# Expert tails in pairs of neighbouring tiles, five PSUM banks in turn, GpSimd's low parts behind VectorE's

## The chip, the cores and the metric

One core of one Trainium2 chip. The metric is the time of one execution on the device, in microseconds; the time of a kernel is the median of its runs.

## What is computed

The kernel chains three layers over 3072 tokens (4 batches of 768) of 320 features: a recurrent attention, a mixture of eight experts that gives each token to one expert, and a gated layer. The change lies in the second.

```python
x = attention output, reshaped to (3072, 320)
for e in range(8):                      # _moe_ref
    mask = expert_idx == e
    h = np.maximum(x[mask] @ w1[e], 0.0)            # 320 -> 1024
    out[mask] = gate_w[mask, None] * (h @ w2[e])    # 1024 -> 320
gate = 1.0 / (1.0 + np.exp(-(x @ w_gate)))          # _moe2_ref
return gate * (x @ w_val) @ w_out
```

## The kernel before, in words

TensorE multiplies in f16, so each f32 operand is split into a high part and a low part (the rest after the high one), and a product takes three matmuls: high by high, high by low, low by high. The program is written in one order by hand; each engine works its own queue in that order, and waits only on semaphores.

**Runs.** The experts are sorted by the number of their tokens. The list `runs` has nine entries: runs 0 and 1 are two halves of the first expert (256 tokens each), runs 2 to 8 one expert each, with windows of 512, 480, 448, 416, 384, 352 and 336 tokens. A run computes with its tokens as the moving columns. The hidden layer of 1024 is eight tiles of 128 units, f = 0 to 7. `expert_run` holds the arithmetic, `expert_steps` puts the work of the other engines between the tiles.

**Layer 1 of a tile** (`l1_tile`): 320 features are two whole blocks of 128 and a tail of 64. A whole block takes three matmuls (L1041, L1042, L1043). For the tail, `w1s` holds the 64 high rows above the 64 low rows, and `x` holds its tail twice, so that two matmuls (L1044, L1045) give all four partial products: 8 matmuls a tile. The results lie in one of PSUM banks 0, 1, 2 in turn. `hidden` then reads the bank twice: ScalarE writes `hh` (L1138), VectorE `hl` (L1139).

**Layer 2** (`expert_l2`) runs two tiles behind: 320 output features are two blocks of 128, three matmuls each (L1054 to L1056), and a tail of 64, whose high and low columns lie side by side in `w2h`, so two matmuls (L1058, L1059) with 128 output rows. `expert_out` adds the two halves of `ys[2]` and stores.

**Between the tiles.** `prepare(f)` refills weights just used with those of the next expert: `split_w1` and `split_w2` are ScalarE copies of the high parts (L221, L244, L258), a VectorE subtraction for the tail's low part (L216) and a GpSimd subtraction for the low part of the whole blocks (L247, L261). The gated layer's f64 weights are split in pieces at the same time (VectorE L1202 to L1219, GpSimd L1223). `load_x` (L767) lets GpSimd gather the token rows of the next run, one block of 128 for each of f = 0 to 3; ScalarE scales a block three tiles later (L1001). At a run's end `transpose_part` turns these rows on TensorE (L1028) into banks 6 and 7 and one of 0 to 2; only as many rows of the last block as the window has. The layer after the experts starts at L1803 with matmuls on half the array's rows (64x128), two at a time.

Of the kernel before, what the change touches and what calls it, by code (L numbers as in the profile page):

```python
# [22 lines left out]
def kernel(  # L23
# [40 lines left out]
    KS, KT, KU = 15, 4, 8  # L64
    SLO, SHI = 2.0 ** -14, 3.99
# [20 lines left out]

    def tp_ps(name):
        return next_bank((6, 7), name)
# [110 lines left out]
    def load_w1(k, p):  # L199

        t = w1r[:, p % 2]
        m, r = t[:, 0:4 * P].rearrange("p (k f) -> p k f", k=2), t[:, 4 * P:6 * P]
        w = w1[expert(k)][0][:, p * 2 * P:(p + 1) * 2 * P]
        nc.sync.dma_start(out=m, in_=w[0:2 * P].rearrange("(k p) f -> p k f", p=P))
        for u in range(2):
            nc.sync.dma_start(out=r[u * RM:(u + 1) * RM], in_=w[2 * P:DM])
        wraw[1, k, p] = (m, r)
# [19 lines left out]
    def tail_sub(dst, x, k, y, early):  # L227
        if early:
            return lambda: scaled_copy(x, x, k), lambda: nc.gpsimd.tensor_tensor(
                out=dst, in0=x, in1=y, op=ALU.subtract  # L230
            )
        return lambda: None, lambda: scaled_sub(dst, x, k, y)

    def split_w1(k, p, lo=None):
        m, r = wraw.pop((1, k, p))
        fs = slice(p * 2 * P, (p + 1) * 2 * P)
        e = lo or nc.gpsimd

        lower = slice(RM, P)
        pre, sub = tail_sub(w1s[lower, fs], r[lower], KT, w1s[lower, fs], k == 0 and lo is None)  # L240

        return [
            lambda: (scaled_copy(w1s[:, fs], r, KT), pre()),
            lambda: nc.scalar.copy(w1h[:, :, fs], m),  # L244
        ], [
            sub,
            lambda: e.tensor_tensor(out=w1l[:, :, fs], in0=m, in1=w1h[:, :, fs], op=ALU.subtract),  # L247
        ]

    def split_w2(k, p, lo=None):  # L250
# [784 lines left out]
    def l1_tile(ps, ws, xt, f):  # L1035

        hi, lo, st = ws
        h, l = xt
        fs = slice(f * P, (f + 1) * P)
        for kk in range(2):  # L1040
            nc.tensor.matmul(ps, hi[:, kk, fs], h[:, kk], start=(kk == 0), stop=False)  # L1041
            nc.tensor.matmul(ps, hi[:, kk, fs], l[:, kk], start=False, stop=False)  # L1042
            nc.tensor.matmul(ps, lo[:, kk, fs], h[:, kk], start=False, stop=False)  # L1043
        nc.tensor.matmul(ps, st[:, fs], h[:, 2], start=False, stop=False)  # L1044
        nc.tensor.matmul(ps, st[:, fs], l[:, 2], start=False, stop=True)  # L1045

    def ring(tag):
        return mw.tile([P, NM], F16, tag=tag, name=tag, bufs=3)

    def expert_l2(ys, hh, hl, f):  # L1050
        first, last = f == 0, f == NF1 - 1
        for d in range(2):
# [3 lines left out]
            nc.tensor.matmul(ys[d], wl, hh, start=False, stop=last)  # L1056
        wr = w2h[:, f, 2 * P:]
# [65 lines left out]
    def expert_run(n):  # L1123
# [326 lines left out]
    last_part, last_low = [], []  # L1450
    PIECES = ((), (), (4,), (2, 4, 6), (2, 4, 6), (2, 4), (2, 4), (4,), (4,))

    def expert_steps(n):
# [7 lines left out]
        def refill(f, u, e, p, lo=None):  # L1461

            if e < NE:
                copies, lows = (split_w1, split_w2)[u](e, p, lo)
                acts[f] += copies
                rest[f].append(lows)
                e, p = (e, p + 2) if p < 2 else (e + 1, p - 2)
                if e < NE:
                    loads[f].append(lambda: (load_w1, load_w2)[u](e, p))

        def prepare(f):
            if n == 1:
# [31 lines left out]
        for f in range(NF1):  # L1504
# [3 lines left out]
            if more and f < len(blocks(n + 1)):  # L1508
                load_x(n + 1, (f,))
# [6 lines left out]
            weave(*rest[f])  # L1516
            weave(ends[f])
# [246 lines left out]

    for n in range(2, len(runs)):
# [43 lines left out]
    sync = mybir.DependencyInfo(mybir.DependencyClass.Sync, mybir.DependencyReason.DATA)  # L1809
# [46 lines left out]
    def gated_h(t, s):  # L1856
        gh, gl = (mw.tile([P, NM], F16, tag=z, name=z, bufs=3) for z in ("hh", "hl"))
# [540 lines left out]
```

## Time and profile before

| what | us |
|---|---|
| median of 3 runs | 706.83 (705.7 to 707.31) |
| the profiled execution | 709.01 |
| its span, first to last instruction | 707.0 |
| runs 2 to 8 in that span | 166.24 to 336.17 |
| the gated layer | 336.17 to 707.0 |

The span is what the trace shows; 2.0 us of the profiled execution lie around it. TensorE is busy in 96% of the span, VectorE in 60%, ScalarE in 59% and GpSimd in 46%. A TensorE row of the trace lasts longer than the step to the next one, since matmuls are pipelined: what a matmul costs is read from start to start.

### The profile page before, as it was taken

Reading aid. Unit: us, or ns where it says so; the run is one execution under the profiler, and the core shown is the slowest. Engines: PE = TensorE matmul, PEld = TensorE weight load, DVE = VectorE, ACT = ScalarE, POOL = GpSimd, SP = SyncE. Lnnn points to the kernel's source line nnn. Section 1 sums busy time; section 2 is a strip of 40 time slices with the busy share of each in tenths; the row PEclk is TensorE's granted clock in tenths of the full one; section 3 lists DMA queues with packets and bytes.
Section 4 is the critical chain, followed back from the end, with each engine's and each line's share of the span. In section 5 each row is a group of like instructions: output and inputs, shape, how many; then the busy total and the mean of one; then the engine's idle time right before and its main releaser. Section 6 shows DMA issues by size and latency. Waiting matters only on the chain. (4 is left out here: it accounts for less than half of the span.)

```text
span 707.0 us, 17947 instructions
## 1 busy us (share of the span) xinstructions
PE 681.2 (96%) x6955; PEld 428.1 (61%) x6955; DVE 424.8 (60%) x928; ACT 419.7 (59%) x1063; POOL 328.1 (46%) x392
## 2 busy tenths in 40 slices
PE   6999999999999999999999999999999999999994
PEld 6899998885445556666555555545544555555552
DVE  7978888797789999887898873343211122211111
ACT  5887886866966677778665554455455453333332
POOL 8968888543754766674010005343243324324222
PEclk9999999999999999999999999999999999999998
DMA  7655875555445566651223211010010001001001
GB/s 231 212 190 180 276 223 160 150 170 162 138 149 177 162 197 191 197 163 57 57 84 88 63 57 40 1 39 1 2 38 2 1 2 38 2 2 39 1 2 41
DMA packets 39865, 70.47 MB, mean 100 GB/s; under 512 B 4818, under 2 KB 28460, under 8 KB 39772
## 3 DMA queue, kind: packets, MB, share of 16 engines
q1 hardware_dynamic: 36764, 59.61, 28.2%
q0 software_dynamic: 3008, 9.64, 4.2%
q8 instruction: 56, 0.92, 0.6%
q14 instruction: 37, 0.30, 0.2%
HBM read 60.55 MB, written 8.68 MB: 98 GB/s over the span
## 5 line engine op out<-in xcount | busy, mean ns | idle before, releaser
L1848 DVE SCALAR_TENSOR_TENSOR sgm<-v_ps,sgm 128x512 f32<-128x512 f32 (+1 forms) x74 | 49.9, 676 | 201.8 <-ACT sgm L1847 201.8
L1861 POOL TENSOR_TENSOR hl<-sgm,hh 128x512 f16<-128x512 f32 x54 | 62.4, 1159 | 214.2 <-ACT hh L1860 214.1
L1803 PE MATMUL v_ps<-xg,wvh 64*128 64x512 f16 x290 | 108.8, 375 | 3.9 <-ACT seen L1817 3.8
L1803 PE MATMUL g_ps<-xg,wgh 64*128 64x512 f16 x290 | 108.8, 375 | 0.0
L1804 PE MATMUL g_ps<-xg,wgh 64*128 64x512 f16 x290 | 108.6, 375 | 0.0
L1804 PE MATMUL v_ps<-xg,wvh 64*128 64x512 f16 x290 | 108.6, 375 | 0.0
L1805 PE MATMUL g_ps<-xg,wgl 64*128 64x512 f16 x290 | 108.6, 375 | 0.0
L1805 PE MATMUL v_ps<-xg,wvl 64*128 64x512 f16 x290 | 108.6, 375 | 0.0
L1847 ACT ACTIVATE sgm<-g_ps 128x512 f32<-128x512 f32 (+1 forms) x74 | 43.1, 585 | 73.1 <-PE g_ps L1805 70.4
L1884 PE MATMUL o_ps<-wo,hh 64*128 64x320 f16 x560 | 84.9, 296 | 1.4 <-ACT seen L1817 1.4
L1886 PE MATMUL o_ps<-wo,hl 64*128 64x320 f16 x560 | 84.8, 296 | 0.5 <-POOL hl L1861 0.5
L1885 PE MATMUL o_ps<-wo,hh 64*128 64x320 f16 x560 | 84.9, 296 | 0.0
L1860 ACT CAST hh<-sgm 128x512 f16<-128x512 f32 (+1 forms) x74 | 44.8, 606 | 43.2 <-DVE sgm L1848 42.2
L1817 ACT COPY seen<-zeros 1x1 f32<-1x1 f32 x142 | 26.8, 188 | 67.6 <-PE o_ps L1886 37.2
L1055 PE MATMUL y_ps<-hl,w2h 128*128 128x256 f16 (+7 forms) x144 | 46.8, 325 | 1.7 <-DVE hl L1139 1.7
L1043 PE MATMUL h_ps<-xh,w1l 128*128 128x256 f16 (+7 forms) x144 | 47.4, 329 | 0.0
L1042 PE MATMUL h_ps<-xl,w1h 128*128 128x256 f16 (+7 forms) x144 | 47.3, 329 | 0.0
L1041 PE MATMUL h_ps<-xh,w1h 128*128 128x256 f16 (+7 forms) x144 | 47.3, 328 | 0.0
L247 POOL TENSOR_TENSOR w1l<-w1raw,w1h 128x512 bf16<-128x512 f32 x31 | 37.6, 1211 | 20.8 <-ACT w1h L244 19.7
L1054 PE MATMUL y_ps<-hh,w2h 128*128 128x256 f16 (+7 forms) x144 | 46.8, 325 | 0.0
L1056 PE MATMUL y_ps<-hh,w2l 128*128 128x256 f16 (+7 forms) x144 | 46.8, 325 | 0.0
L479 PE MATMUL s_ps<-qk 40*128 40x128 f32 (+1 forms) x384 | 42.1, 300 | 4.5 <-DMA qk<-in_qkt_dram 4.3
(383 smaller groups left out, 1963.1 us busy)
## 6 DMA issues: line engine op xcount, KB each, us to landing
kv<-in_kvo_dram SPq DMA_DIRECT2D x24, 484.0 KB
w2raw<-in_moe_w_dram SPq DMA_DIRECT2D x32, 320.0 KB
w1raw<-in_moe_w_dram SPq DMA_DIRECT2D x32, 256.0 KB
qk<-in_qkt_dram SPq DMA_DIRECT2D x48, 160.0 KB
xs<-x SPq DMA_DIRECT2D x24, 192.0 KB
w1raw<-in_moe_w_dram SPq DMA_DIRECT2D x64, 64.0 KB
raw<-in_moe_w_out_dram SPq DMA_DIRECT2D x12, 320.0 KB
raw<-in_moe_w_gate_dram SPq DMA_DIRECT2D x8, 384.0 KB
```

The source lines that it names most:

```text
L1041: nc.tensor.matmul(ps, hi[:, kk, fs], h[:, kk], start=(kk == 0), stop=False)
L1042: nc.tensor.matmul(ps, hi[:, kk, fs], l[:, kk], start=False, stop=False)
L1043: nc.tensor.matmul(ps, lo[:, kk, fs], h[:, kk], start=False, stop=False)
L1054: nc.tensor.matmul(ys[d], wh, hh, start=first, stop=False)
L1803: lambda: nc.tensor.matmul(ps, at(wh), h[rows, kk], start=start, stop=False),
L1804: lambda: nc.tensor.matmul(ps, at(wh), l[rows, kk], start=False, stop=False),
L1805: lambda: nc.tensor.matmul(ps, at(wl), h[rows, kk], start=False, stop=stop),
L1848: nc.vector.scalar_tensor_tensor(out=s[:, cs], in0=pv[:, cs], scalar=2.0 ** -KH, in1=s[:, cs], op0=ALU.mult, op1=ALU.mult)
L1861: e.tensor_tensor(out=gl[:, cs], in0=s[:, cs], in1=gh[:, cs], op=ALU.subtract)
L1884: lambda: nc.tensor.matmul(o, gh[rows, ts_], wh[rows], start=begin, stop=False),
L1885: lambda: nc.tensor.matmul(o, gh[rows, ts_], wl[rows], start=False, stop=False),
L1886: lambda: nc.tensor.matmul(o, gl[rows, ts_], wh[rows], start=False, stop=end),
```

## The change

For runs 2 to 8 it multiplies the tails of two neighbouring tiles together. In `w1s` the 64 high rows of an even tile now lie above those of the odd tile, the low rows likewise in the next 128 columns, and each tile's three tail products use one half of the array's rows, the two tiles alternating (`l1_tails`). They come ahead of the tile's other products, for four tiles at once, at f = 0 and f = 4. In layer 2 the tails of two tiles use one half of the array's columns each (`l2_tails`), at f = 4 for tiles 0 and 1 and after the last tile for the rest, so `hh` and `hl` get six buffers (three before, also in the gated layer). Tiles, transposes and the small products of runs 2 to 8 take banks 0, 1, 2, 6, 7 in turn. From the third expert on each GpSimd low part waits for the VectorE subtraction recorded last. The tail's f32 rows are loaded without doubling, so its ScalarE copy handles 128x128 elements (before 128x256) and its VectorE subtraction 128x128 (before 64x256). `load_x` stands behind the tile's splits instead of ahead of them, row blocks are turned whole, and the tail of the last layer-2 refill moves into the next run (`kept`).

```diff
     def load_w1(k, p):
...
+            if k:
+                nc.sync.dma_start(out=r[rows, 0:P], in_=w[2 * P:DM, u * P:(u + 1) * P])
...
+    def holds(op):
+        port[:] = [op()]
+    def yields(ins):
+        if port:
+            tc.add_manual_dep(ins.ins, port[0].ins.name, sync, reason="VectorE goes first")
+        return ins
...
-        return lambda: None, lambda: scaled_sub(dst, x, k, y)
+        return lambda: None, lambda: holds(lambda: scaled_sub(dst, x, k, y))
+    def low_op(k, ins, e):
+        if k > 1 and e is nc.gpsimd:
+            yields(ins)
...
+        if k:
+            hi, lw = (w1s[:, (2 * p + v) * P:(2 * p + v + 1) * P] for v in range(2))
+            r = r[:, 0:P]
+            pre, sub = tail_sub(lw, r, KT, hi, False)
...
-            m = min(P, s0 + w - j * P)
-            o, xr = tp[:, u * P:u * P + m], xrow[n][0:m, u, kk * P:(kk + 1) * P]
-            nc.tensor.transpose(o, xr, ident[0:m, 0:m])
+            nc.tensor.transpose(tp[:, u * P:(u + 1) * P], xrow[n][:, u, kk * P:(kk + 1) * P], ident)
...
+    def l1_tails(pss, ws, xt, f):
+        h, l = (z[:, 2] for z in xt)
+        def three(ps, rows):
+            hi, lo = (ws[2][rows, (f + v) * P:(f + v + 1) * P] for v in range(2))
+            return [
+                lambda: nc.tensor.matmul(ps, hi, h[rows], start=True, stop=False),
+                lambda: nc.tensor.matmul(ps, hi, l[rows], start=False, stop=False),
+                lambda: nc.tensor.matmul(ps, lo, h[rows], start=False, stop=False),
+            ]
+        alternate(*(three(ps, rows) for ps, rows in zip(pss, half_rows)))
...
+    def l2_tails(ys, hs, f):
+        def three(u):
+            rows, (hh, hl) = half_rows[u], hs[u]
+            hi, lo = (w2h[:, f + u, 2 * P + v * RM:2 * P + (v + 1) * RM] for v in range(2))
+            o = ys[2][rows]
+            return [
+                lambda: nc.tensor.matmul(o, hi, hh, start=(f == 0), stop=False),
+                lambda: nc.tensor.matmul(o, hi, hl, start=False, stop=False),
+                lambda: nc.tensor.matmul(o, lo, hh, start=False, stop=(f == NF1 - 2)),
+            ]
+        alternate(three(0), three(1))
...
+                if f == 4:
+                    l2_tails(ys, [h.pop(u) for u in range(2)], 0)
+                if f % 4 == 0:
+                    for u in range(0, 4, 2):
+                        for v in range(2):
+                            pss[f + u + v] = tp_ps("h_ps")[:, 0:w]
+                        l1_tails([pss[f + u + v] for v in range(2)], ws, x, f + u)
+                l1_main(pss[f], ws, x, f, False, True)
...
+        if n > 1:
+            for f in range(2, NF1, 2):
+                l2_tails(ys, [h.pop(f + u) for u in range(2)], f)
...
-            if more and f < len(blocks(n + 1)):
-                load_x(n + 1, (f,))
             prepare(f)
...
             weave(*rest[f])
+            if more and f < len(blocks(n + 1)):
+                load_x(n + 1, (f,))
...
+    tp_banks[0] = (0, 1, 2, 6, 7)
     for n in range(2, len(runs)):
```

On TensorE, where run 2 begins, the first tile before had its tail behind the whole blocks (`w1s` is the tail's weights, `w1h` and `w1l` those of the whole blocks):

```order
L1041 LDWEIGHTS w1h
L1041 MATMUL h_ps<-xh,w1h 128x512
L1042 LDWEIGHTS w1h
L1042 MATMUL h_ps<-xl,w1h 128x512
L1043 LDWEIGHTS w1l
L1043 MATMUL h_ps<-xh,w1l 128x512
L1044 LDWEIGHTS w1s
L1044 MATMUL h_ps<-xh,w1s 128x512
L1045 LDWEIGHTS w1s
L1045 MATMUL h_ps<-xl,w1s 128x512
```

Now run 2 begins with the tails of tiles 0 and 1, of which this is the first pair:

```order
L1099 LDWEIGHTS w1s
L1099 MATMUL h_ps<-xh,w1s 128x512
L1099 LDWEIGHTS w1s
L1099 MATMUL h_ps<-xh,w1s 128x512
L1100 LDWEIGHTS w1s
L1100 MATMUL h_ps<-xl,w1s 128x512
L1100 LDWEIGHTS w1s
L1100 MATMUL h_ps<-xl,w1s 128x512
L1101 LDWEIGHTS w1s
L1101 MATMUL h_ps<-xh,w1s 128x512
L1101 LDWEIGHTS w1s
L1101 MATMUL h_ps<-xh,w1s 128x512
```

Each line stands twice, once for each tile; the third token block `xh`, `xl`, which was needed last, is needed first.

On TensorE at f = 4 of run 2, what is now between the last whole-block product of layer 2 (L1129) and the tails of tiles 4 and 5 (L1099):

```order
L1129 MATMUL y_ps<-hh,w2l 128x512
L1116 LDWEIGHTS w2h
L1116 MATMUL y_ps<-hh,w2h 64x512
L1116 LDWEIGHTS w2h
L1116 MATMUL y_ps<-hh,w2h 64x512
L1117 LDWEIGHTS w2h
L1117 MATMUL y_ps<-hl,w2h 64x512
L1117 LDWEIGHTS w2h
L1117 MATMUL y_ps<-hl,w2h 64x512
L1118 LDWEIGHTS w2h
L1118 MATMUL y_ps<-hh,w2h 64x512
L1118 LDWEIGHTS w2h
```

Six matmuls with 64 output rows each stand in a row; whole array, column halves, row halves and whole array follow one another.

On GpSimd in run 3 before, each gather of token rows (L767) stood ahead of its tile's low part (L247, L261):

```order
L767 DMA xrow<-xs,idx 128x384
L247 TENSOR_TENSOR w1l<-w1raw,w1h 128x2x256
L767 DMA xrow<-xs,idx 128x384
L261 TENSOR_TENSOR w2l<-w2raw,w2h 128x512
L767 DMA xrow<-xs,idx 128x384
L247 TENSOR_TENSOR w1l<-w1raw,w1h 128x2x256
L767 DMA xrow<-xs,idx 128x384
L261 TENSOR_TENSOR w2l<-w2raw,w2h 128x512
```

Now each stands behind it (L798 is the gather, L278 and L292 the low parts):

```order
L278 TENSOR_TENSOR w1l<-w1raw,w1h 128x2x256
L798 DMA xrow<-xs,idx 128x384
L292 TENSOR_TENSOR w2l<-w2raw,w2h 128x512
L798 DMA xrow<-xs,idx 128x384
L278 TENSOR_TENSOR w1l<-w1raw,w1h 128x2x256
L798 DMA xrow<-xs,idx 128x384
L292 TENSOR_TENSOR w2l<-w2raw,w2h 128x512
L798 DMA xrow<-xs,idx 128x384
```

So a gather waits for whatever its tile's low part waits for.

## Rows read from the trace of the kernel before

**Rows 1.** Windows, runs 5, 8: length; PE, PEld, DVE, ACT, POOL busy; clock; DMA
```profile
251.92:275.45 23.53, 23.53 (x138) 13.53 (x137) 22.94 (x36) 16.82 (x45) 15.30 (x15) 1.00 0.61 179
...
317.83:336.17 18.34, 18.34 (x130) 12.43 (x128) 12.93 (x26) 14.31 (x37) 8.45 (x8) 1.00 0.18 55
```
**Rows 2.** Timeline of TensorE, run 2, one layer-2 tile of eight matmuls: start, duration
```profile
171.52 0.38 PE L1054 MATMUL y_ps<-hh,w2h 128*128 128x512 f16 x1
...
173.24 0.38 PE L1041 MATMUL h_ps<-xh,w1h 128*128 128x512 f16 x1
```
**Rows 3.** Timeline of TensorE, end of run 8 and start of the gated layer
```profile
333.65 0.31 PE L1059 MATMUL y_ps<-hl,w2h 128*128 128x336 f16 x1
...
335.93 0.31 PE L1059 MATMUL y_ps<-hl,w2h 128*128 128x336 f16 x1
336.17 0.39 PE L1803 MATMUL g_ps<-xg,wth 64*128 64x512 f16 x1
336.18 0.39 PE L1803 MATMUL v_ps<-xg,wth 64*128 64x512 f16 x1
336.40 0.38 PE L1804 MATMUL g_ps<-xg,wth 64*128 64x512 f16 x1
```
**Rows 4.** Timeline of TensorE, attention: column halves (128x64); the x2 row: last two alone
```profile
42.49 0.27 PE L598 MATMUL tp_x<-ident,x 128*128 128x128 f32 x1
42.70 0.66 PE L529 MATMUL u_ps<-vw,kv 128*64 128x41 f32 x16
43.29 0.38 PE L479 MATMUL s_ps<-qk 128*128 128x128 f32 x1
...
43.07 0.29 PE L529 MATMUL u_ps<-vw,kv 128*64 128x41 f32 x2
```
**Rows 5.** Timeline of TensorE near the end: row halves, then the whole array
```profile
693.78 0.30 PE L1886 MATMUL o_ps<-wo,hl 64*128 64x320 f16 x2
694.01 0.31 PE L1905 MATMUL o_ps<-wo,hh 128*128 128x320 f16 x1
```
**Rows 6.** Timeline of TensorE: turning rows for run 2 (512) and run 4 (448)
```profile
160.86 1.47 PE L1028 MATMUL tp_m<-ident,xrow 128*128 128x128 f32 x12
162.17 0.27 PE L1054 MATMUL y_ps<-hh,w2h 128*128 128x256 f16 x1
...
220.56 2.05 PE L1028 MATMUL tp_m<-ident,xrow 128*128 128x128 f32 x12
222.55 0.38 PE L1054 MATMUL y_ps<-hh,w2h 128*128 128x480 f16 x1
```
**Rows 7.** Lines of VectorE, 166 to 336 us: busy us, mean ns, idle before
```profile
L216 DVE SCALAR_TENSOR_TENSOR w1s<-w1raw,w1s 64x256 f16<-64x256 f32 x25 | 18.7, 747 | 2.2 <-ACT w1s L221 1.5
```
**Rows 8.** Timeline of run 5, TensorE, VectorE and GpSimd: tile 3 from matmul to use
```profile
258.78 0.34 PE L1045 MATMUL h_ps<-xl,w1s 128*128 128x416 f16 x1
...
264.81 0.34 PE L1055 MATMUL y_ps<-hl,w2h 128*128 128x416 f16 x1
...
258.39 1.91 DVE L216 SCALAR_TENSOR_TENSOR w1s<-w1raw,w1s 64x256 f16<-64x256 f32 x1
...
264.17 0.58 DVE L1139 SCALAR_TENSOR_TENSOR hl<-h_ps,hh 128x416 f16<-128x416 f32 x1
...
266.54 0.42 DVE L216 SCALAR_TENSOR_TENSOR w1s<-w1raw,w1s 64x256 f16<-64x256 f32 x1
...
258.84 1.16 POOL L261 TENSOR_TENSOR w2l<-w2raw,w2h 128x512 bf16<-128x512 f32 x1
```
**Rows 9.** Timeline of run 5, GpSimd and ScalarE: first gather, first low part, first scaling
```profile
252.15 1.30 POOL L767 DMA_INDIRECT xrow<-xs,idx  x1
...
256.37 1.34 POOL L247 TENSOR_TENSOR w1l<-w1raw,w1h 128x512 bf16<-128x512 f32 x1
...
259.66 0.60 ACT L1001 ACTIVATE xrow<-xrow,gsl 128x384 f32<-128x384 f32 x1
```
**Rows 10.** Timeline of TensorE, end of run 2: the product that spreads the gate weights
```profile
193.36 1.12 PE L1010 MATMUL sp_ps<-dg,ones_f 128*128 128x512 f32 x2 [0.58 <-DVE xl L216]
```

More of the change, by code (lines that the diff above doesn't have):

```diff
@@ L85, in mm_ps @@
         return next_bank((0, 1, 2, 3), name)
+    tp_banks = [(6, 7)]
     def tp_ps(name):
-        return next_bank((6, 7), name)
+        return next_bank(tp_banks[0], name)
     def o_ps(j):
@@ L1033, in transpose_part, with l1_main @@
         scaled_sub(l, tp[:, o:o + w], up, h)
-    def l1_tile(ps, ws, xt, f):
-        hi, lo, st = ws
+    def l1_main(ps, ws, xt, f, first, last):
+        hi, lo, _ = ws
         h, l = xt
@@ L1047, in ring, with l1_tile @@
-    def ring(tag):
-        return mw.tile([P, NM], F16, tag=tag, name=tag, bufs=3)
-    def expert_l2(ys, hh, hl, f):
+            nc.tensor.matmul(ps, lo[:, kk, fs], h[:, kk], start=False, stop=(last and kk == 1))
+    def l1_tile(ps, ws, xt, f):
+        l1_main(ps, ws, xt, f, True, False)
+        st = ws[2][:, f * P:(f + 1) * P]
+        h, l = xt
+        nc.tensor.matmul(ps, st, h[:, 2], start=False, stop=False)
+        nc.tensor.matmul(ps, st, l[:, 2], start=False, stop=True)
+    half_rows = [slice(u * RM, (u + 1) * RM) for u in range(2)]
@@ new lines, in alternate @@
+    def alternate(*chains):
+        for ops in zip(*chains):
+            for op in ops:
+                op()
+    def l1_tails(pss, ws, xt, f):
[8 more added lines that the diff above has]
+        alternate(*(three(ps, rows) for ps, rows in zip(pss, half_rows)))
@@ new lines, in ring @@
+    def ring(tag):
+        return mw.tile([P, NM], F16, tag=tag, name=tag, bufs=NH_)
+    def l2_tails(ys, hs, f):
[9 more added lines that the diff above has]
+        alternate(three(0), three(1))
@@ L1056, in expert_l2 @@
             nc.tensor.matmul(ys[d], wl, hh, start=False, stop=last)
+    def expert_l2(ys, hh, hl, f):
+        first, last = f == 0, f == NF1 - 1
+        l2_main(ys, hh, hl, f)
         wr = w2h[:, f, 2 * P:]
@@ L1450 @@
     last_part, last_low = [], []
+    kept = []
     PIECES = ((), (), (4,), (2, 4, 6), (2, 4, 6), (2, 4), (2, 4), (4,), (4,))
@@ L1464, in refill @@
                 copies, lows = (split_w1, split_w2)[u](e, p, lo)
+                e, p = (e, p + 2) if p < 2 else (e + 1, p - 2)
+                load = [lambda: (load_w1, load_w2)[u](e, p)] if e < NE else []
+                if n > 1 and u and f == NF1 - 1:
+                    kept.append((copies[0:1], lows[0:1], load))
+                    copies, lows, load = copies[1:], lows[1:], []
                 acts[f] += copies
                 rest[f].append(lows)
-                e, p = (e, p + 2) if p < 2 else (e + 1, p - 2)
-                if e < NE:
-                    loads[f].append(lambda: (load_w1, load_w2)[u](e, p))
+                loads[f] += load
         def prepare(f):
+            if f == 0 and kept:
+                a, b, c = kept.pop()
+                acts[f] += a
+                rest[f].append(b)
+                loads[f] += c
             if n == 1:
@@ L1856, in gated_h @@
     def gated_h(t, s):
-        gh, gl = (mw.tile([P, NM], F16, tag=z, name=z, bufs=3) for z in ("hh", "hl"))
+        gh, gl = (mw.tile([P, NM], F16, tag=z, name=z, bufs=NH_) for z in ("hh", "hl"))
         e = nc.vector if t == last or ready or todo else nc.gpsimd
```

49 lines of the change are left out of this document (31 added, 18 removed).

## Prediction

> **What bounds the kernel now.** The page's shares name TensorE, but a pipelined engine can look busy and yet wait, and a share is a mean over stages. So the first view is the windows by stretch: in runs 5 and 8 TensorE's busy time equals the length of the stretch and the granted clock is 1.00, its 2.4 GHz level [rows 1]. The timeline settles it. In run 2 one tile of layer 2 takes 173.24 - 171.52 = 1.72 us for eight matmuls, 0.215 each [rows 2]. At the end of run 8 sixteen matmuls take 335.93 - 333.65 = 2.28 us, 0.1425 each [rows 3]. The reader should see equal steps with nothing between them: runs 2 to 8 are a sum of TensorE slots, and a slot removed is time gained, as long as the operands come in time. The second thing to see is how near the other engines are. VectorE is busy for 22.94 of run 5's 23.53 us [rows 1], and one row shows the edge: tile 3's last product starts at 258.78, its `hl` is done at 264.17 + 0.58 = 264.75, and layer 2 reads it at 264.81 [rows 8]. That is 34 slots of cover, used up.
>
> **Slots removed.** A pair of tiles has four tail matmuls in layer 1 and four in layer 2. If two halves of the array run together, three steps replace four in each. Four pairs and two layers make 8 slots a run. A slot is 0.1425 us at 336 columns and 0.215 at 512, so 0.00041 us a column between; the seven windows add up to 2928 columns, and one slot of each run to 7 x 0.1425 + (2928 - 7 x 336) x 0.00041 = 1.234 us. Eight make **-9.9 us**.
>
> Do two halves run together? For row halves at 512 columns the two rows start 0.01 apart and the next pair 0.22 later [rows 3]: yes, at the price of one slot. For column halves the case shows only short f32 products: the last two, on the same half, stand 0.29 - 0.23 = 0.06 apart (0.23 is one row's length: the second starts at 43.13 and ends with the sixteen at 43.36), and sixteen take 43.13 + 0.06 - 42.70 = 0.49 us, where one after the other they would take 0.96 [rows 4]. So they overlap about twofold. That f16 products of 336 to 512 columns do so too is carried over, not seen. The bounds for a column pair are one slot and two; I take one.
>
> **Changes of mode added.** From the whole array to row halves the last slot is 336.17 - 335.93 = 0.24 instead of 0.14, and the first pair takes 0.01 more than a slot [rows 3]: 0.11. From row halves back, 694.01 - 693.78 = 0.23 for a slot of some 0.136 (320 columns, by the same line): 0.10 [rows 5]. Into column halves 42.70 - 42.49 = 0.21 for a transpose that takes 1.31 / 12 = 0.11 [rows 4, 6]: 0.10. Out of them the last product starts at 43.13, is worth 0.06, and its successor starts at 43.29: 0.10 [rows 4]. A run now has six changes (row halves at f = 0 and back, columns, rows and back at f = 4, columns at the end); of the 42 the last takes the place of the one into the gated layer. 41 x 0.105 = **+4.3 us**. The bounds are 0.10 and a whole drain: a row lasts 0.31 and its step is 0.1425 [rows 3], so 0.17 would be exposed, 7.0 us in all.
>
> The Trainium skill speaks against the change here: TensorEngine Tiling (Array Packing), Key Properties, says that a change of tiling mode, not of tile, drains the engine. Rows 3 show a loss, but of 0.11 instead of the 0.17 of a whole drain; by the rule read strictly the gain would shrink by 2.7 us.
>
> **Whole row blocks.** Twelve transposes of whole blocks take 162.17 - 160.86 = 1.31; with a last block of 64 rows 222.55 - 220.56 = 1.99, because each short block switches the array's mode [rows 6]. Run 4 gains 0.68; run 5 (last block 32 rows) by estimate 0.6; runs 3, 7 and 8 (96, 96, 80 rows) lose by estimate 0.08, 0.08 and 0.12, three blocks each by the missing share of 0.11. **-1.0 us.**
>
> **Banks.** At the end of run 2 the spreading product waits 0.58 for a bank that `xl` still reads [rows 10]. With five banks in turn it gets tile 7's, read earlier: -0.3, between 0 and -0.6. Against that, four tiles take their banks at once. Tile 7's bank was tile 2's, 25 slots after that tile; where a small product (counts, places) has taken one, it is tile 3's, 13 slots after it, or the third transpose takes tile 7's after 7 slots and eight transposes: 2 to 3 us, while run 5's tile 3 needed 264.75 - 258.78 = 6.0 [rows 8]. That is three places in seven runs.
>
> **Cover for the other engines.** Tiles 4 and 5 now have 26 slots until `hl` is read, 4.6 us in run 5, instead of 34. VectorE gets lighter: its `w1s` subtraction takes 0.42 us undisturbed, 0.75 on average and 1.91 at worst [rows 7, 8], the worst lying across a GpSimd low part that began 0.45 after it. It halves in columns, and GpSimd waits for it, so 25 subtractions lose the 18.7 - 25 x 0.42 = 8.2 us of waiting, part of which moves on to the next VectorE operation.
>
> GpSimd pays: behind its low part now stands the gather. In run 5 the first gather began at 252.15; behind the low part at 256.37 + 1.34 it begins at 257.7, and ScalarE scales these rows at 259.66 [rows 9], sooner now. A gather takes 1.0 to 1.3 us to issue and must land after that, so ScalarE will wait 1 to 3 us at f = 3 in runs 4 and 5, and `hh` and `hl` of tile 4 behind it. The nine slots of tails that TensorE has at f = 4 (1.6 us in run 5) cover most of it. The third token block, now read first, has 21 slots between its transposes and its use, 3.0 us at the least, where twelve transposes' copies took about that; I count nothing for it. The `kept` tail is read at the end of the next run only, a whole run of cover. Banks, gathers and shorter cover together: **+1.5 us**, between 0 (VectorE relieved enough) and 5.
>
> **Sum.** -9.9 + 4.3 - 1.0 - 0.3 + 1.5 = -5.4 us. The profiled execution would go from 709.0 to 703.6; it is 2.2 above the median, so the median goes from 706.8 to **701.4**.
>
> **Rivals.** *VectorE becomes the bound (0.14).* In run 5 it is at 22.94 / 23.53 = 97%; if it can't be fed better and its work shrinks by nothing, run 5 gains nothing, and I let runs 3 and 4, where it is nearly as full, go with it. Their share of the gain is 8 x (0.20 + 0.19 + 0.175) = 4.5, less 18 changes (1.9), plus the transposes' 1.2: 3.8 us lost, 1.5 of them counted already: 703.7; 704.4 if run 6 joins, and up to 706 where waits for `hl` come on top. For it speaks the read at 264.81 [rows 8]; against it that half of the long subtractions' time was waiting.
>
> *Whole drains (0.07)*: +2.7, 704.1. Against it stand three kinds of change measured at 0.10.
>
> *Column pairs do not overlap (0.06).* Then a pair's six layer-2 products take six slots instead of three: 3 x 4 x 1.234 = +14.8 us, 716.2, slower. It decides from half: if a pair costs 1.36 slots the 5.4 us are gone. For it speaks that two moving streams of 128 rows at f16 speed occur nowhere in this trace; against it the twofold overlap of the short products [rows 4].
>
> *Better than forecast (0.08).* No new wait, the spreading product free, and run 1's short waits for VectorE gone: 698.5 to 699.5.
>
> **How the numbers follow.** The forecast has 0.65 and spans 699.5 to 704. With the better case, the drains and the VectorE bound, 698.5 to 705.3 holds the time 8 times in 10 and more; the column case stays outside. Runs of one kernel differ by about 0.2%, 1.4 us, which is what a measurement can tell from no change. Faster takes the forecast, the better case, the drains and more than half of the VectorE case: 0.65 + 0.08 + 0.07 + 0.08 = 0.88. 0.05 of that case is the same; its last 0.01 and the columns are slower, 0.07.
>
> **What would show it.** Runs 2 to 8 should last about 164.5 us instead of 169.9. Each row pair and each column pair of tails should step by one slot (0.22 at 512, 0.14 at 336); a column pair of 0.3 or more in run 8 makes the forecast wrong. Six steps a run should be longer by 0.10; 0.17 means whole drains. Transposes of runs 4 and 5 should take 1.31. The `w1s` subtraction should be near 0.3 us, and GpSimd's low parts should start where it ends. ScalarE should wait at L1001's successor in runs 4 and 5 for the gather. Any TensorE idle time over 0.3 us in runs 3 to 6 that ends with `hl` says that VectorE took over, and more than 5 us of it in all that I was wrong about the cover. The gated layer should be as long as before, 370.8 us.

## The result, and the profile after

The changed kernel is slower, by less than 1%: 711.27 us (median of 6; 709.62 to 713.93) against 706.27 for the kernel before, with a recorded ratio of 1.0083 [1.0054, 1.0111] (the two medians alone give 1.0071). Timed again on another chip it was 1.0059 [1.0035, 1.0083]. 701.4 had been forecast. The profiled execution took 713.5 us, with a span of 711.5.

The stages, from each one's first product: runs 0 and 1 take 33.8 us instead of 35.2, runs 2 to 8 take 179.2 instead of 169.9, and what follows 366.5 instead of 370.8. (The first of them starts at 132.0 instead of 131.0.) Here are runs 3 to 8 and their sum, in the columns of [rows 1]:

```profile
198.90:226.05 27.15, 26.55 (x159) 12.86 (x159) 25.14 (x44) 17.32 (x45) 15.88 (x14) 1.00 0.52 156
226.05:255.57 29.52, 26.60 (x160) 13.06 (x158) 25.56 (x38) 17.89 (x47) 16.47 (x15) 0.94 0.57 167
255.57:280.19 24.62, 23.19 (x156) 12.41 (x155) 20.60 (x32) 16.25 (x45) 15.57 (x14) 1.00 0.54 159
280.19:303.82 23.63, 21.80 (x157) 12.46 (x156) 19.85 (x34) 15.45 (x44) 14.82 (x13) 1.00 0.58 175
303.82:324.71 20.89, 20.03 (x156) 12.42 (x155) 14.27 (x27) 14.25 (x42) 13.26 (x12) 1.00 0.48 145
324.71:344.98 20.27, 18.57 (x146) 11.40 (x144) 13.76 (x26) 14.17 (x38) 8.42 (x7) 1.00 0.16 50
sum 146.08, PE 136.74 PEld 74.61 DVE 119.17 ACT 95.34 POOL 84.43; mean PE 22.79 PEld 12.43 DVE 19.86 ACT 15.89 POOL 14.07
```

In [rows 1] TensorE's busy time equalled the length of run 8, 18.34 us. Now it is 18.57 of 20.27, and in run 5 it is 23.19 of 24.62: TensorE waits. VectorE is less busy than before (20.60 us in run 5 instead of 22.94). It doesn't look like an engine that has run out of time.

The slots and mode changes came out as forecast. TensorE at the start and at the end of run 8:

```profile
324.71 0.32 PE L1099 MATMUL h_ps<-xh,w1s 64*128 64x336 f16 x2
324.86 0.30 PE L1100 MATMUL h_ps<-xl,w1s 64*128 64x336 f16 x2
325.00 0.30 PE L1101 MATMUL h_ps<-xh,w1s 64*128 64x336 f16 x2
...
325.43 0.30 PE L1101 MATMUL h_ps<-xh,w1s 64*128 64x336 f16 x2
325.67 0.32 PE L1073 MATMUL h_ps<-xh,w1h 128*128 128x336 f16 x1
...
343.34 0.31 PE L1129 MATMUL y_ps<-hh,w2l 128*128 128x336 f16 x1
343.58 0.33 PE L1116 MATMUL y_ps<-hh,w2h 128*64 128x336 f16 x2
...
344.46 0.31 PE L1116 MATMUL y_ps<-hh,w2h 128*64 128x336 f16 x2
344.60 0.31 PE L1117 MATMUL y_ps<-hl,w2h 128*64 128x336 f16 x2
344.74 0.31 PE L1118 MATMUL y_ps<-hh,w2h 128*64 128x336 f16 x2
344.98 0.39 PE L1907 MATMUL g_ps<-xg,wth 64*128 64x512 f16 x1
```

Row pairs (`64*128`, x2) step by 0.14 to 0.15. Column pairs (`128*64`, x2) step by 0.14, one slot: two halves of the columns do run together at f16 and 336 columns, which the trace before had not shown. Back from the row halves the slot is 325.67 - 325.43 = 0.24, into the columns 343.58 - 343.34 = 0.24, and from the columns to row halves 344.98 - 344.74 = 0.24: 0.10 for a change above the slot of 0.1425, as counted. Twelve transposes for run 4 now take 220.82 - 219.51 = 1.31 instead of 1.99:

```profile
219.51 1.47 PE L1060 MATMUL tp_m<-ident,xrow 128*128 128x128 f32 x12
220.82 0.37 PE L1127 MATMUL y_ps<-hh,w2h 128*128 128x480 f16 x1
```

So by its slots this stage should last 169.9 - 9.9 + 4.3 - 1.0 = 163.3 us. It lasts 15.9 longer. What TensorE waited for in runs 2 to 8 (us in all, times, longest):

```profile
PE y_ps L1128 <- DVE hl L1219: 7.8, 10, 2.3
PE sp_ps L1041 <- DVE hl L1219: 1.8, 1, 1.8
PE tp_m L1060 <- DVE hl L1219: 0.9, 1, 0.9
PE h_ps L1099 <- DVE hl L1219: 0.9, 1, 0.9
PE y_ps L1127 <- ACT hh L1218: 0.5, 1, 0.5
```

These rows see 11.9 us; a wait shorter than a matmul's modelled length is partly hidden in them. All but one end with `hl`, VectorE's half of the hidden tile; 3.6 us of them (`sp_ps`, `tp_m`, `h_ps`) are waits for a bank that `hl` still reads. One wait is dearer than its length. Run 4, TensorE, then the stretch in which the clock fell:

```profile
248.64 0.35 PE L1127 MATMUL y_ps<-hh,w2h 128*128 128x448 f16 x1
251.27 0.53 PE L1128 MATMUL y_ps<-hl,w2h 128*128 128x448 f16 x1 [2.28 <-DVE hl L1219]
251.59 0.58 PE L1129 MATMUL y_ps<-hh,w2l 128*128 128x448 f16 x1
251.97 0.58 PE L1127 MATMUL y_ps<-hh,w2h 128*128 128x448 f16 x1
```
```profile
251.50:254.20 2.70, 2.70 (x11) 0.98 (x11) 2.60 (x6) 0.00 (x0) 0.20 (x1) 0.50 0.27 80
```

After 2.28 us of idleness the granted clock is 0.50, the 1.2 GHz level, and a slot is 251.97 - 251.59 = 0.38 instead of 0.19 until 254.3.

### The profile page after: what moved, and what is told of

The parts are those of the page before. It is cut to its first block, busy times and chain, and to the rows that moved or that the text cites. A ratio compares the mean times of both kernels' runs of the same rounds, so it can differ in the third digit from the quotient of the medians.

```text
span 711.5 us, 18194 instructions
## 1 busy us (share of the span) xinstructions
PE 678.9 (95%) x7067; PEld 429.0 (60%) x7067; DVE 419.6 (59%) x928; ACT 415.4 (58%) x1063; POOL 327.5 (46%) x392
## 5 line engine op out<-in xcount | busy, mean ns | idle before, releaser
L1987 PE MATMUL o_ps<-wo,hh 64*128 64x320 f16 x560 | 86.1, 296 | 0.0
L1988 PE MATMUL o_ps<-wo,hh 64*128 64x320 f16 x560 | 86.1, 296 | 0.0
L1920 ACT COPY seen<-zeros 1x1 f32<-1x1 f32 x142 | 26.8, 189 | 64.9 <-PE o_ps L1989 34.9
L278 POOL TENSOR_TENSOR w1l<-w1raw,w1h 128x512 bf16<-128x512 f32 x31 | 37.7, 1217 | 30.4 <-ACT w1h L275 8.9
L1219 DVE SCALAR_TENSOR_TENSOR hl<-h_ps,hh 128x256 f16<-128x256 f32 (+7 forms) x72 | 39.5, 549 | 20.5 <-ACT hh L1218 20.2
L1129 PE MATMUL y_ps<-hh,w2l 128*128 128x256 f16 (+7 forms) x144 | 47.2, 328 | 0.0
```

The source lines that it names most:

```text
L1987: lambda: nc.tensor.matmul(o, gh[rows, ts_], wh[rows], start=begin, stop=False),
L1988: lambda: nc.tensor.matmul(o, gh[rows, ts_], wl[rows], start=False, stop=False),
```

## First round of experiments: gathers, and GpSimd's wait

Theory A: the gathers, issued late, make ScalarE and so `hl` late. Rival B: the cover of 26 slots is too short. Rival C: the five banks. Rival D: GpSimd's low parts wait for VectorE. Four kernels; before was 712.53 us on their chip.

**Gathers first, as before the change.**
```diff
+            if more and f < len(blocks(n + 1)):
+                load_x(n + 1, (f,))
             prepare(f)
...
-            if more and f < len(blocks(n + 1)):
-                load_x(n + 1, (f,))
```


> The change, with the gathers of token rows ahead of the tile's splits again (load_x where it was before). Theory A (the gather stands behind a low part, lands late, ScalarE waits for it at f = 3, and hh, hl and the matmuls behind it are late): ScalarE's waits for the gather go from 13.2 us to under 1, TensorE's waits for hl from 7.8 us to under 3, runs 2 to 8 from 179.2 us to 166 to 171, the time to 0.985 to 0.995 of before. Rival B (the shorter cover between a tile and its use makes the wait, whatever the gathers do): ScalarE's waits go, but hl stays late by 5 us or more and runs 2 to 8 stay above 175. Rival C (five banks in turn): waits for banks stay and are most of what is lost, about 4 us.


Ratio to before 1.0053 [1.0032, 1.0074]. ScalarE's waits for gathers, 13.2 us in nine waits, are gone, yet TensorE's for `hl` are 6.5 us and runs 2 to 8 last 178.7. Run 7 gained 1.3 us (20.89 to 19.59) and run 2 lost as much (33.1 to 34.4); over runs 3 to 8 the gain is 1.8. Theory A explains little.

**No wait of GpSimd.**
```diff
-        if k > 1 and e is nc.gpsimd:
-            yields(ins)
+        return
```


> The change, without GpSimd's waits for VectorE (the gathers stay behind the low parts). Theory A: GpSimd's first low part of a run waits for ScalarE's copy anyway, so the gathers land as late as in the change, ScalarE still waits 10 us or more for them, and the time is within 2 us of the change. Rival D (GpSimd's wait for VectorE holds its queue and the gathers with it): ScalarE's waits fall below 6 us and the time falls by 4 us or more. If the lock on the shared port was what the wait saves, w1s subtractions go from 0.59 us on average to over 0.7.


1.0076 [1.0051, 1.0101]; `hl` 7.3 us, runs 2 to 8 179.0, and ScalarE still waits 13.6 us for gathers. The `w1s` subtraction took 0.58 us on average, against 0.59 with the wait, so the wait saves nothing there. Run 4 is 1.6 us shorter than in the changed kernel and run 2 1.7 longer, both with the granted clock (run 4 1.00 instead of 0.94, run 2 0.95 instead of 1.00). **Both together:**


> The change with both undone: gathers first, no waits of GpSimd for VectorE. Theory A: within 2 us of e1, since the wait for VectorE matters little once the gathers are out of its way. Rival D: faster than e1 by 2 us or more. If the wait for VectorE is worth its keep, slower than e1 by 1 us or more, with longer w1s and w2h subtractions.


1.0085 [1.0061, 1.0110]; 179.3. Rival D falls.

**The kernel before with late gathers only.**


> The kernel before with only the gathers moved behind the splits. Theory A: ScalarE waits for gathers here too, some 5 to 13 us, and because each tile had 34 slots of cover instead of 26 the time rises, but by less than in the change: 1.001 to 1.010 of before. Rival B: no change of time, since the cover alone decides.


0.9996 [0.9979, 1.0012]. ScalarE waits 7.2 us for gathers, but runs 2 to 8 stay at 170.2: in the old order late gathers cost nothing.

## Second round: cover, load, buffers

Rival E: VectorE has too much to do in runs 3 to 6, whenever its results are read.

**Before with six buffers for `hh` and `hl`**, since the gated layer had become 4.3 us shorter with unchanged code.
```diff
-        return mw.tile([P, NM], F16, tag=tag, name=tag, bufs=3)
+        return mw.tile([P, NM], F16, tag=tag, name=tag, bufs=6)
...
```


> The kernel before with one edit: six instead of three buffers for the hidden halves (hh, hl), in the experts and in the gated layer. Theory 1, the buffers make the gated layer 4 us shorter in the changed kernel (366.5 against 370.8 us): here too the gated layer lasts about 366.5 us, runs 2 to 8 stay at 170 us, and the ratio to before is about 0.994. Theory 2, that difference is what two executions differ by: the gated layer stays at 371 us within 2 us and the ratio is 0.998 to 1.002.


0.9998 [0.9981, 1.0016]: nothing. When the changed kernel was profiled again (below), its gated layer took 370.3 us: the 366.5 is a difference between executions.

**Layer 2 three tiles behind.**
```diff
-                if f == 4:
+                if f == 5:
                     l2_tails(ys, [h.pop(u) for u in range(2)], 0)
...
-            if f >= 2:
-                l2(f - 2)
+            lag = 2 if n < 2 else 3
+            if f >= lag:
+                l2(f - lag)
...
```


> The changed kernel with layer 2 three tiles behind layer 1 instead of two in runs 2 to 8 (the column pair of tiles 0 and 1 moves from f = 4 to f = 5, which adds one change of mode a run, +0.7 us). A tile's hl is then read 12 slots later. Rival B (the cover is too short, VectorE has the time but not soon enough): TensorE's waits for hl fall from 7.8 to under 2 us, runs 2 to 8 from 179 to 165 to 170 us, the ratio to before is 0.985 to 0.996. Rival E (VectorE as a whole has too much to do in runs 3 to 6, whenever its results are read): the waits move to later tiles and to the banks, hl and bank waits stay above 5 us, runs 2 to 8 above 176 us, ratio 1.004 to 1.012.


1.0158 [1.0134, 1.0183]. I had expected this to repair the kernel. Every tile had 12 slots more cover and runs 2 to 8 took 184.7 us. Layer 2's waits for `hl` fell from 7.8 to 3.7 us, but others took their place (`tp_m` for `hl` 3.0 us, a small product 2.0), and most of the loss lies in run 2 (37.8 instead of 33.1, its granted clock 0.91). Runs 3 to 8, at a clock of 1.00, took 146.9 us instead of 146.1: more cover gained them nothing. Rival B, my own reason so far, falls.

**Weight pieces later.**
```diff
-    PIECES = ((), (), (4,), (2, 4, 6), (2, 4, 6), (2, 4), (2, 4), (4,), (4,))
+    PIECES = ((), (), (4,), (4,), (4,), (2, 4, 6), (2, 4, 6), (2, 4), (2, 4))
```


> The changed kernel with the weight pieces of the gated layer (five VectorE operations, two ScalarE operations each) moved: runs 3 and 4 prepare one each instead of three, runs 5 and 6 three instead of two, runs 7 and 8 two instead of one. Without waits run 3 should last 26.3, run 4 24.7, run 5 22.9, run 6 21.3, run 7 19.5, run 8 17.9 us by the slots. Rival E (VectorE's load): runs 3 and 4 come down from 27.15 and 29.52 to about these, and runs 5 to 8 get longer by 1 to 2 us each; total 708 to 714, ratio 0.998 to 1.006. Rival B (cover for each single hl, whatever the load): runs 3 and 4 keep gaps of 0.5 to 2 us at hl and shorten by less than a third of their waits (under 1.9 us together); ratio 1.006 to 1.012.


1.0194 [1.0168, 1.0221]. Runs 3 and 4 of this kernel:
```profile
198.27:224.65 26.38, 26.38 (x160) 12.86 (x159) 17.36 (x34) 15.78 (x42) 14.34 (x13) 1.00 0.48 145
224.65:249.33 24.68, 24.68 (x160) 12.77 (x158) 15.48 (x27) 16.07 (x43) 14.23 (x13) 1.00 0.52 156
```
26.38 and 24.68 us with no idle time: exactly the 26.3 and 24.7 of the slots. Runs 5 to 8 each got 2.7 to 3.0 longer for one piece more (runs 5 and 8 with a granted clock of 0.94 and 0.93, runs 6 and 7 at 1.00). The work of the other engines inside a run sets its length, as rival E says, though run 8 suffers with VectorE busy for 13.76 of 20.27 us. **Behind, even and first together:**


> The changed kernel with layer 2 three tiles behind, the 13 pieces spread evenly (one in run 2, two in each of runs 3 to 8) and the gathers issued before the low parts. If cover and load are together what failed: hardly any wait for hl is left (under 1 us), runs 2 to 8 last 164 to 167 us, and the ratio to before is 0.980 to 0.992. If banks or other waits take over: runs 2 to 8 stay above 172 us, ratio above 0.998.


1.0184 [1.0159, 1.0208], runs 2 to 8 185.4 (run 2 38.6, runs 3 to 8 146.8): my expectation failed again.

## Third round: a stretch of fixed length

These runs suggested another cut. In each run take the time from the first product to the first `hh` (ahead), from there to the end of the last `hl` (stretch), and on to the next run's first product (behind), all read from the three engines' timelines:

| run | before: ahead / stretch / behind | changed | e9 (below) |
|---|---|---|---|
| 3 | 1.82 / 22.39 / 3.82 | 2.75 / 21.30 / 3.10 | 2.14 / 21.43 / 3.47 |
| 4 | 1.77 / 22.47 / 1.88 | 2.59 / 22.58 / 4.35 | 2.02 / 22.59 / 1.78 |
| 5 | 1.67 / 20.10 / 1.77 | 2.43 / 19.47 / 2.73 | 1.90 / 19.47 / 2.27 |
| 6 | 1.56 / 18.12 / 2.74 | 2.33 / 18.38 / 2.92 | 1.84 / 18.38 / 3.44 |
| 7 | 1.45 / 15.55 / 2.97 | 2.17 / 16.37 / 2.35 | 1.72 / 16.61 / 1.87 |
| 8 | 1.40 / 15.26 / 1.68 | 2.09 / 15.93 / 2.26 | 1.66 / 15.92 / 1.41 |
| sum | 9.67 / 113.88 / 14.85 | 14.34 / 114.03 / 17.72 | 11.27 / 114.40 / 14.23 |

The stretch didn't get shorter by the slots taken out of it: 113.9 and 114.0 us. Run by run it fell by up to 1.1 us or rose by up to 0.8, so that the two sums agree this closely is partly chance. Counted from the rows of the traces, TensorE's busy time inside the six stretches fell from 113.7 to 104.9 us, while at least one of ScalarE and VectorE was busy for 113.0 of the 113.9 us before and for 112.7 of the 114.0 after. With layer 2 three tiles behind the stretch was 114.4. **Theory W**: ScalarE and VectorE, each waiting for the other in a fixed order, need this stretch whatever TensorE does in it. What TensorE does ahead of it and behind it is added.

Ahead now stand the tails of four tiles, behind it the tails of six: 4.7 and 2.9 us more. Run 8 shows the order from inside, ScalarE, VectorE, GpSimd and TensorE:

```profile
337.39 0.43 ACT L1218 ACTIVATE hh<-h_ps 128x336 f16<-128x336 f32 x1
...
340.47 0.51 ACT L1316 CAST wgh<-fa 128x384 f16<-128x384 f32 x1 [2.55 <-DVE fa L1313]
341.00 0.63 ACT L1843 ACTIVATE sq<-yT 64x512 bf16<-64x512 f32 x1
341.54 0.43 ACT L1218 ACTIVATE hh<-h_ps 128x336 f16<-128x336 f32 x1
...
337.51 1.38 DVE L1845 TENSOR_TENSOR sqs<-sqs,sq 64x512 bf16<-64x512 bf16 x1
338.82 0.49 DVE L1219 SCALAR_TENSOR_TENSOR hl<-h_ps,hh 128x336 f16<-128x336 f32 x1
339.24 0.54 DVE L1310 SCALAR_TENSOR_TENSOR fb<-raw,fb 128x384 int32<-128x384 int32 x1
339.88 0.56 DVE L1313 SCALAR_TENSOR_TENSOR fa<-fb,fa 128x384 int32<-128x384 int32 x1
...
337.04 1.58 POOL L245 TENSOR_TENSOR xg<-yT,xg 128x512 f16<-128x512 f32 x1 [0.25 <-ACT xg L244]
...
342.23 0.30 PE L1127 MATMUL y_ps<-hh,w2h 128*128 128x336 f16 x1 [0.46 <-ACT hh L1218]
```

Tile 7's relu (341.54) stands behind the piece's copy `wgh`. That waits 2.55 us for `fa`, which on VectorE stands behind a squaring that took 1.38 us while GpSimd was busy until 338.62, behind tile 6's `hl`, and behind `fb`. TensorE comes last. The Trainium skill's PSUM — Partial Sum Buffer, Engine vs sequencer instructions, calls these engines' queues strict FIFO. The trace agrees: tile 7's relu starts only after the copy and the squaring ahead of it.

**Tails where TensorE waits**: layer-1 tails pair by pair, and at the end the tails of tiles 2 to 5 ahead of layer 2 of tile 6.
```diff
-                if f % 4 == 0:
-                    for u in range(0, 4, 2):
...
+                if f % 2 == 0:
+                    for v in range(2):
+                        pss[f + v] = tp_ps("h_ps")[:, 0:w]
+                    l1_tails([pss[f + v] for v in range(2)], ws, x, f)
...
+        if n > 1:
+            for f in (2, 4):
+                l2_tails(ys, [h.pop(f + u) for u in range(2)], f)
         if n:
             l2(NF1 - 2)
             l2(NF1 - 1)
         if n > 1:
-            for f in range(2, NF1, 2):
-                l2_tails(ys, [h.pop(f + u) for u in range(2)], f)
+            l2_tails(ys, [h.pop(NF1 - 2 + u) for u in range(2)], NF1 - 2)
```


> The changed kernel with the tails moved to where TensorE waits: layer-1 tails are taken pair by pair (in front of tiles 0, 2, 4, 6) instead of four tiles at once, and of the layer-2 tails at a run's end those of tiles 2 to 5 go ahead of layer 2 of tile 6. It adds six changes of mode a run (+4.2 us in all if TensorE is the bound). Theory W (from a run's first relu to its last hl ScalarE and VectorE need a fixed time, 114 us in all over runs 3 to 8 both before and after; TensorE work ahead of it and behind it adds to it): the window stays at 112 to 116 us, the time ahead of it falls by 3 slots a run (3.1 us over runs 3 to 8) and the time behind it by about 5.5 us, run 2 comes to about 31.5; runs 2 to 8 last 168 to 171 us instead of 179, ratio to before 0.996 to 1.002. Rival B (each hl lacks cover, wherever the tails stand): the waits stay and the changes of mode come on top, runs 2 to 8 last 180 to 184 us, ratio 1.010 to 1.018.


0.9933 [0.9912, 0.9954], 706.15 us against 710.6: faster than before by more than I had expected, and, by the repetition below, than the changed kernel, with six changes of mode a run more. Runs 2 to 8 last 170.3 us, the stretch 114.4. It keeps the five banks in turn, so rival C falls too. TensorE's waits in these runs are down to
```profile
PE tp_m L1060 <- DVE perm L1450: 1.2, 1, 1.2
PE y_ps L1128 <- DVE hl L1219: 1.1, 2, 0.9
```

**Run 8's squarings moved into the gated layer.**
```diff
-            if n == len(runs) - 1:
-                checks.pop(0)()
...
+        if t < 4:
+            checks.pop(0)()
+            checks.pop(0)()
```


> The changed kernel with the eight squarings of row sums that run 8 does (0.63 us of ScalarE each, most with 0.4 to 1.4 of VectorE) moved into the first four tiles of the gated layer. Theory W: run 8's window from the first relu to the last hl falls from 15.9 to about 13, and the run from 20.3 to its slots, 17.9 to 18.4 us; runs 2 to 7 as before; the gated layer 0 to 1 us longer; ratio to before 1.003 to 1.008. Rival B (cover): the piece's round trip still makes hl late, run 8 stays above 19.5 us.


1.0071 [1.0046, 1.0096]: run 8's stretch falls from 15.93 to 13.78 and the run from 20.28 to 18.13 us, though `hl` has no more cover than before. (The gated layer pays: 373.4 us, with new gaps of 1.49 and 0.97 in its first tiles. Run 2 took 34.8 us with unchanged code; see the front-half and end-tail kernels below.) **All of these, and better shares of pieces:**


> The two edits before together, with the gathers issued ahead of the low parts, and the 13 pieces given to the runs whose TensorE time is longest against their window (1, 3, 2, 2, 2, 1, 2 in runs 2 to 8). Theory W: windows of 24.7, 18.7, 18.3, 18.3, 15.1 and 15.6 us in runs 3 to 8 stay within TensorE's own time or just above; runs 2 to 8 last 166 to 169 us, the gated layer 0 to 1 us more, ratio to before 0.990 to 0.998. If waits for banks or the changes of mode are what is left: over 172 us, ratio above 1.002.


0.9992 [0.9979, 1.0005]: runs 2 to 8 169.4, with the gated layer's loss of 3 us. Both missed what I had expected. The stretch fell to 106.6 us, but the time behind it rose to 20.0: TensorE's own work, with its six more changes of mode a run, was nearly the bound again. **The same moves in the kernel before:**


> A control: the kernel before with the squarings moved and the pieces given to the runs as in the run above, and nothing of the change. Theory W with TensorE as the bound of before: runs 2 to 8 stay at 169 to 171 us, since no wait was there to be removed; ratio 0.998 to 1.003. If before too was held by the other engines, it gains: below 168 us, ratio under 0.997.


1.0036 [1.0020, 1.0051], with the gated layer's loss of 3 us; runs 2 to 8 169.9, as ever. There the stretch fell from 113.9 to 109.3 and the time behind it rose by 4.6: TensorE was the bound at the same time, as I had read it.

## Fourth round: which end, and is the inside free?

> Only the first half of e9_tails_inside: layer-1 tails pair by pair, layer-2 tails at the end as in the changed kernel. Four changes of mode more a run. Theory W: the time ahead of the first relu falls by 3.1 us over runs 3 to 8, the windows stay at 114, the time behind the last hl at 17.7; runs 2 to 8 last 174.5 to 176.5 us (179.2 in the changed kernel); ratio to before 0.999 to 1.005. If TensorE's slots and changes were the bound: 182 us, ratio 1.012.


1.0017 [1.0002, 1.0031], against a before of 705.1; runs 2 to 8 171.1, better than expected. The time ahead fell by the 3.1 us, run 2 by 3.0 (its wait for a bank at `sp_ps` is gone), and run 4's clock stayed at 1.00.


> Only the second half of e9_tails_inside: the layer-2 tails of tiles 2 to 5 ahead of layer 2 of tile 6. Two changes of mode more a run. Theory W: the time behind the last hl falls by 3.5 us over runs 3 to 8, the rest of them stays, run 2 falls by about 1.5; runs 2 to 8 last 173.5 to 175.5 us; ratio 0.998 to 1.004. If TensorE's slots and changes were the bound: 180.6 us, ratio 1.010.


1.0058 [1.0043, 1.0073]; 176.2, both above what I had expected. The time behind fell by 5.0 over runs 3 to 8, but run 2 took 34.9. Run 2 in the changed kernel, then here:
```profile
165.80:198.90 33.10, 30.43 (x166) 13.57 (x165) 20.37 (x40) 25.69 (x59) 18.16 (x17) 1.00 0.45 140
165.84:200.75 34.91, 32.24 (x166) 13.73 (x164) 20.34 (x40) 25.68 (x59) 18.36 (x17) 0.95 0.44 133
```
The same wait of 1.8 us at `sp_ps` left the granted clock at 1.00 in the changed kernel and was followed by a lower one here, as in the kernels without GpSimd's wait and with the squarings moved (34.8 us each). Where the wait is gone, as in the front-half kernel, run 2 took 30.1.

**Four slots a run more inside the stretch**, the low products of tiles 2 and 4 taken twice.
```diff
+            if n > 2 and f in (4, 6):
+                for d in range(2):
+                    wl = w2l[:, f - 2, d * P:(d + 1) * P]
+                    nc.tensor.matmul(ys[d], wl, h[f - 2][0], start=False, stop=False)
```


> The changed kernel with four TensorE slots added to each of runs 3 to 8 inside the window: at f = 4 and f = 6 the products of the low weights of tile f - 2 are taken a second time (they are then counted twice in the output). By the slots this is 4 x 1.02 = 4.1 us more. Theory W (TensorE waits there for ScalarE and VectorE anyway): runs 3 to 8 stay at 146 to 147.5 us and the ratio to before at 1.006 to 1.011, as that of the changed kernel. If TensorE's work there is on the path: runs 3 to 8 last 150 us and the ratio is 1.012 to 1.017.


1.0111 [1.0087, 1.0135]. Runs 5 and 8, and the sum of runs 3 to 8:
```profile
255.98:280.60 24.62, 23.89 (x161) 12.81 (x161) 20.60 (x32) 16.36 (x45) 15.57 (x14) 1.00 0.56 158
...
325.13:345.40 20.27, 19.05 (x152) 11.79 (x152) 13.75 (x26) 14.29 (x38) 8.16 (x7) 1.00 0.17 50
sum 146.09, PE 140.20 PEld 76.96 DVE 119.23 ACT 95.69 POOL 84.69; mean PE 23.37 PEld 12.83 DVE 19.87 ACT 15.95 POOL 14.12
```
146.09 us against 146.08, with 3.5 us more of TensorE's busy time. 4.1 us of slots were added without making these runs longer. This is the plainest evidence for theory W. The ratio, 1.0111, doesn't decide by itself: it lies between the two I had named, and the changed kernel was not timed beside it.

**Repetitions on one chip** (before 711.98).


> The same kernel as e9_tails_inside once more, beside the changed kernel on one chip. Theory W: runs 2 to 8 last 170 to 171 us and the kernel is 8 to 9 us faster than the changed kernel on this chip. Against before, whose runs 2 to 8 last 169.9, the slots' stage explains a ratio of 1.000 and the shorter run 1 (34 instead of 35.3 us) one of 0.998; if 0.9933 comes again, a stage outside runs 1 to 8 is faster too; if it is 0.998 to 1.003, the 0.9933 held for that chip only.


0.9954 [0.9936, 0.9972], 709.16 us, runs 2 to 8 169.7.


> The changed kernel itself on the same chip as the two others: ratio to before 1.0055 to 1.011, runs 2 to 8 last 179 us.


1.0059 [1.0035, 1.0083], 716.70 us, runs 2 to 8 179.2: the tails' places are worth 7.5 us.

**A fourth piece in run 3.**


> e9_tails_inside with one weight piece moved from run 6 to run 3, which then prepares four and run 6 one. Theory W: run 3's window grows from 21.4 by about 2 us into time that TensorE has there, so the run lasts 27 to 27.6 instead of 27.0; run 6's window falls by 3, so the run lasts 21.6 to 22 instead of 23.65; 1 to 1.6 us less than e16_inside_again in all (0.2%). If a fourth piece delays run 3 by a piece's 2.5 us, nothing is gained or 0.1% lost.


1.0019 [1.0001, 1.0037]. Run 6 fell to 21.96 as expected, but run 3 took 33.4 instead of 27.0. TensorE waited 3.37 us there, once, and then ran at the lower clock:
```profile
216.91 0.40 PE L1401 MATMUL pm_ps<-ident,tf 128*32 128x128 f32 x1 [3.37 <-DVE tf L1437]
```
```profile
217.00:222.90 5.90, 5.90 (x19) 1.94 (x20) 4.58 (x10) 3.05 (x8) 1.25 (x1) 0.50 0.60 178
```
```profile
211.85 0.18 DVE L1434 TENSOR_SCALAR tf<-ipo 128x32 f32<-128x32 f32 x1
...
214.61 2.25 DVE L1437 TENSOR_TENSOR tf<-tf 128x32 f32<-128x32 f32 x1
```
A product of the list of places stands in TensorE's queue and needs a tiny VectorE result behind the pieces. The wait and 5.9 us at half the clock make up the 6.4.

## Why the prediction was wrong

**What bounds the kernel** is the step that failed: "runs 2 to 8 are a sum of TensorE slots, and a slot removed is time gained, as long as the operands come in time". In before TensorE waited for only 0.8 us in runs 2 to 8, and so I missed that the other engines' chain, from a run's first relu to its last `hl`, was equally long: ScalarE or VectorE was busy for 113.0 of its 113.9 us. Slots taken from that stretch left TensorE waiting in it; slots collected ahead of it and behind it were paid in full. The 7.7 us that runs 3 to 8 grew by are 4.7 ahead, 2.9 behind (1.4 of them run 4's lower clock: 4.35 us instead of 2.92 in the front-half kernel) and 0.15 in the stretch; run 2 adds 1.6.

**Cover for the other engines**, +1.5 with banks and gathers (0 to 5), was the term mis-sized by this: 15.9 us. I counted cover tile by tile and took VectorE's relief for time won. Its `w1s` subtraction fell to 0.59 us on average, not 0.3, and part of the time saved went into the pieces. Before:
```profile
L1205 DVE TENSOR_SCALAR fb<-raw 128x384 int32<-128x384 int32 x13 | 18.1, 1395 | 0.0
L1219 DVE SCALAR_TENSOR_TENSOR fa<-fb,fa 128x384 int32<-128x384 int32 x13 | 10.4, 802 | 0.5
L1208 DVE SCALAR_TENSOR_TENSOR fb<-raw,fb 128x384 int32<-128x384 int32 x13 | 7.7, 590 | 0.5
```
After (L1302 was L1208, L1313 was L1219, L223 was L216):
```profile
L1302 DVE SCALAR_TENSOR_TENSOR fb<-raw,fb 128x384 int32<-128x384 int32 x13 | 17.5, 1347 | 0.4
L1313 DVE SCALAR_TENSOR_TENSOR fa<-fb,fa 128x384 int32<-128x384 int32 x13 | 16.3, 1257 | 0.7
L223 DVE SCALAR_TENSOR_TENSOR w1s<-w1raw,w1s 128x128 f16<-128x128 f32 x25 | 14.9, 594 | 2.1 <-ACT w1s L241 2.1
```
L1205 (now L1299) fell to 737 ns, the other two rose. All five operations of the pieces took 59.4 us instead of 52.9, while the tails' subtractions (`w1s`, `w2h`) fell from 35.4 to 25.6.

The *VectorE* rival had the engine and my threshold (over 5 us of waits for `hl`) told it. But it allowed a run only to lose its gain, and put the loss at 706 at most; that tails ahead and behind make a run longer than before was in no case.

**Slots, changes of mode, transposes** were right in size, and the two rivals on them are out. **The spreading product's bank** was wrong in sign: 1.76 us of idleness instead of 0.58, since the bank was tile 7's, whose `hl` was late. **Gathers**: ScalarE's wait came, up to 2.9 us, but was mostly beside the path.

The repaired order could not have kept the forecast's gain either: its six more changes of mode a run cost 42 x 0.105 = 4.4 us by estimate, so by its slots runs 2 to 8 come to 163.3 + 4.4 = 167.7 us, 2.2 less than before.

The repaired kernel is 0.5 to 0.7% faster than before although its runs 2 to 8 are as long (170.3 and 169.7 against 169.9). Runs 0 and 1 give some of it (34.1 and 33.9 us, against 34.8 to 35.6 in the four profiles of kernels of the old form): TensorE's waits for `hl` there, 1.7 us before, fell to 0.2 or less, as the *Better than forecast* rival had it. Where the rest lies is open: what follows run 8 differs by up to 4 us between profiles of one kernel.

## What to carry to other kernels

When one engine never waits, that doesn't say that the others have slack: read, per stage, how long their own chain takes from its first input to its last output, and for how much of that at least one of them is busy. If it equals the stage, work removed from the busy engine gains nothing there. It must come from the chain too, and what is moved should go to places where the engine would wait, not in front of the chain's start or behind its end.

## Unexpected of the hardware

- Column pairs at f16 run fully together: a step of 0.14 us at 336 columns for two matmuls. Each change of mode measured between the whole array, row halves and column halves costs about 0.10 us, whichever two it joins, less than the 0.17 of a whole drain (a row's length of 0.31 less its step of 0.1425).
- The same wait of TensorE, 1.8 us in front of the same product, left the granted clock of run 2 at 1.00 in both profiles of the changed kernel (33.1 us) and was followed by a mean of 0.95 in three other kernels (34.8 to 34.9 us).
- A VectorE operation of 128x32 elements took 2.25 us with GpSimd at work nearly all that time; the same operation took 0.18 in the repaired kernel. The Trainium skill's SBUF — State Buffer, SBUF: two separate sides, describes an exclusive port lock between the two engines, which a VectorE operation needs when it has two SBUF inputs or runs in a two-port mode. The trace agrees in so far as this operation has two inputs and ends at 216.86, 0.06 after the second of two GpSimd subtractions in a row (216.80). Two inputs are not needed for such a wait: in before, `tf<-ipo` (L1339), which has one and took 0.17 in the changed kernel, took 1.13 and ended at 210.36, 0.02 after GpSimd's low part (L261). Which mode it ran in no trace shows.
